# Weights from float64: the sign by a slope of ScalarE, every low part on VectorE

## The chip, the cores and the metric

The kernel runs on one core of a Trainium2 chip. The metric is the device time of one execution, in microseconds. PE is TensorE, DVE is VectorE, ACT is ScalarE, POOL is GpSimd, SP is SyncE, whose queue issues all the transfers here.

## What is computed

A banded attention of 4 batches and 8 heads (576 positions of 64), half of the heads with a dilation of 4, then two feed-forward layers over the 2304 tokens. Cut to what matters:

```
scores = q @ k.T / 8, masked to a band of 32 positions (heads 4 to 7: every 4th of 128)
x = softmax(scores) @ v                        # 2304 tokens x 512
h = x @ w_in;  x = (h * sigmoid(h)) @ w_out    # 512 -> 2048 -> 512
out = (((x @ w1) * (x @ w2)) @ w3) @ w_out2    # 512 -> 1024 -> 1024 -> 512
```

The inputs q, k, v are float32, the weights float64; the result is float32.

## The kernel before

**Products.** A float32 product is made of three faster ones: each operand is split into a high part of fewer bits and a low part (what is missing), and hi*hi, lo*hi and hi*lo are accumulated in PSUM. `split` does it for activations: ACT copies the high part (L452), DVE subtracts (L453).

**Weights.** [...] `Convert` turns a piece of 128 x 512 numbers into float32 by its bits, in a pipeline of stages that are queued as single entries:

- `load`: SP brings the raw piece, 512 KB (L365), into one of four buffers.
- `rebias`: ACT takes the high words (sign, exponent, top of the mantissa) as if they were float32, and multiplies them in place by 2 to the power of -112 (L375), which puts the exponent right.
- `bits`: DVE shifts the high word left by 3 and masks off the sign bit (L383), ORs the sign back in (L387), and ORs in the top three bits of the low word (L391). The float32 number y is done, in one of two buffers.
- `high`: ACT rounds y into the high part, in the weights' place wf (L400).
- `low`: the low part, y minus the high part. For the first layer (`cv`), a piece of odd number goes to POOL (L407), one of even number to DVE (L409). `cv` holds w_in and w_out in turn, so its even pieces are those named i (w_in), its odd ones u (w_out). `cv2`, the second layer's pieces, has them all on DVE.

`fill` queues the entries of the next piece: the low part of an earlier piece, the high part of another, the three bit operations, and the next rescaling, six in all. `micro` takes one entry from the queue, `step` all of them, `need` as many as are wanted for a piece to be complete.

**Order.** The program is emitted in an order that strings of letters set. `START` goes before the first chunk: 12 units of attention (a unit is two blocks of 96 queries for two heads), with conversion entries between. Then come five chunks of tokens through the first layer, with a slot for each of the 16 feature tiles; `SLOT[c]` orders a slot of chunk c. In a slot, h and H are the halves of the next slot's first product (L522, 12 matmuls), t is its nonlinearity (ACT's Tanh, L532, then DVE, L533), g its split, x and X the second product (L550, 12 matmuls); a is a step of the attention, m a conversion entry, c a whole step. Chunk 0 converts two pieces a slot, i and u of a tile; chunks 3 and 4 begin with the second layer's.

A unit of attention runs through these steps, each behind the last: scores on PE (L187), mask and maximum on DVE (L203, 4 instructions with 4 reads of the accumulator), exponentials on ACT (L215, 4), sums and reciprocal on DVE (L223, L225), the normalise on POOL (L227), 4 transposes on PE (L235), their copy on ACT (L241), the product with v on PE (L250, 8 records), and the split into xT (ACT L260, DVE L261).

An engine executes its instructions in the order of the program. `fill` and `low` are where the change lies:

```
if low < high:
    self.queue.append(lambda: self.low(low))
if high < i and high <= self.gate:
    self.queue.append(lambda: self.high(high))
if i < len(self.todo) and i < self.nl + 2:
    self.queue += [lambda x=x: self.bits(i, x) for x in range(3)]
    self.queue.append(lambda: self.rebias(i + 1))
```

Of the kernel before, what the change touches and what calls it, by code (L numbers as in the profile page):

```python
# [17 lines left out]
P = 128  # L18
B, H, S, D = 4, 8, 576, 64
NPAIR = H // 2              # heads go in pairs: 128 partitions of (head, d)  # L20
DM, DFF, DF2 = 512, 2048, 1024
NT = B * S
WIN = 32                    # band width, in (class-ordered) positions
DIL = 4
CL = S // DIL               # positions of a class of a dilated head
QB = 96                     # queries of an attention block
NU = S // (2 * QB)          # units (two blocks) of a pair of heads
PER_B = NPAIR * NU
NUNIT = B * PER_B
KW = 224                    # keys of a unit  # L30
# [3 lines left out]
RING = 1280                 # tokens that xT holds  # L34
CH1 = [(0, 512), (512, 512), (1024, 256), (1280, 512), (1792, 512)]
CH2 = [(0, 512), (512, 512), (1024, 512), (1536, 512), (2048, 256)]
R2 = [0, 512, 0, 512, 1024]  # where a chunk of the second layer lies in xT

# The order of emission. A step of the attention is a group of operations, each with the
# lag (in units) at which it runs behind the first one:  # L40
#   Q split q and k   S scores   M mask and maximum   E exp   N normalise   T transpose
#   W evacuate the transposes   V product with v   O output into xT   K, L load k, v
ATT0 = "S0W2|M0V2|L2T1|K0E0|N0|O2"    # first batch
ATT = "Q0L4K2S1|M1T2|W2E1|V2N1O2"
# Before the first chunk, then in a slot (a feature tile) of each chunk of the first layer:
#   a a step of the attention      m c a part of, a whole step of converting weights
#   h H halves of the next slot's first product     t g its nonlinearity, and its split
#   x X halves of this slot's second product        w W halves of a group of w3 @ wo2
# [10 lines left out]
SPLIT_FROM = 28             # from this unit on the scores are float32r products too  # L59
# [3 lines left out]
# float32 products: each operand is split into hi + lo, two float32r values of  # L63
# 12 significant bits, and hi*hi + lo*hi + hi*lo is accumulated in float32.
# The weights come as float64: their bits are turned into float32 on chip.
# [3 lines left out]
def tile_kernel(  # L69
# [36 lines left out]
    def f32(ap):  # L106
        return ap.bitcast(F32)

    # ---------------------------------------------------------------- masks
    # blocks:  A first block | B inside | C class edge inside | D class edge in front  # L110
    # order of the tile: A B B A C B D
    def build_masks():
# [8 lines left out]
        for i in range(7):  # L121
            lead = 0 if i in (0, 3) else WIN   # 0 <= qi - (kj - lead) < WIN
            keep(mask[:, i, :], lead, 1, -1, P)
            keep(mask[:, i, :], WIN - 1 - lead, -1, 1, P)
        edge = CL - QB                         # class edge inside block 1 (and 4)
# [6 lines left out]
    # ---------------------------------------------------------------- attention  # L132
# [123 lines left out]
    def a_out(n):  # L256
# [6 lines left out]
        def place(a, n_):  # L263
            """cut positions a .. a + n_ of all batches where the ring ends"""
            first = min(n_, RING - a % RING)
            return [(0, first, a % RING)] + ([(first, n_ - first, 0)] if first < n_ else [])

# [31 lines left out]
    def attention_steps():  # L299
        """The steps of the attention, pipelined over units: lists of (operation, unit)."""  # L300
# [12 lines left out]
    class Stream:  # L313
        def __init__(self):
            self.steps, self.at, self.out = attention_steps(), 0, 0
            self.limit = 2 * PER_B          # units whose place in xT is free
# [20 lines left out]
    # ---------------------------------------------------------------- weights  # L337
    # wf[i], first layer: [w_in hi | w_in lo | w_out hi | w_out lo], 512 each
    def quarter(i, k):
        """hi and lo, half k of wf[i]: [P, 2, 512]"""  # L340
# [8 lines left out]
    class Convert:  # L349
        """float64 pieces [P, 512] -> float32 -> hi, lo; a pipeline of four stages."""  # L350

        def __init__(self):
            self.todo = []
            self.nb = self.nh = self.nl = 0     # the next piece of a stage
            self.gate = 1 << 30                 # the last piece whose place is free
# [14 lines left out]
        def rebias(self, i):  # L370
            if i < len(self.todo):
                self.load(i)
                h = self.raw[i][:, :, 1].bitcast(F32)
                # the exponent's offset: 1023 - 127 = 112 * 8, and tiny values go to zero
                nc.scalar.activation(h, h, AF.Copy, scale=2.0 ** -112)  # L375

        def bits(self, i, x):
# [4 lines left out]
            if x == 0:  # L382
                nc.vector.tensor_scalar(  # L383
                    y, hw, 3, 0x7FFFFFF8, op0=ALU.logical_shift_left, op1=ALU.bitwise_and
                )
            elif x == 1:
                nc.vector.scalar_tensor_tensor(  # L387
                    y, hw, -2147483648, y, op0=ALU.bitwise_and, op1=ALU.bitwise_or
                )
# [12 lines left out]
        def low(self, i):  # L402
            if 0 <= i < len(self.todo):
                dst, y = self.parts(i)
                del self.y[i]
                if self is cv and i % 2 == 1:
                    nc.gpsimd.tensor_tensor(dst[:, 1], y, f32(dst[:, 0]), op=ALU.subtract)  # L407
                else:
                    nc.vector.tensor_sub(dst[:, 1], y, f32(dst[:, 0]))  # L409
# [5 lines left out]
        def fill(self):  # L415
# [9 lines left out]
            if i < len(self.todo) and i < self.nl + 2:  # L425
                self.queue += [lambda x=x: self.bits(i, x) for x in range(3)]
# [23 lines left out]
    def split(dst, src):  # L450
        """dst [P, 2, n] <- hi, lo of src [P, n]"""
# [404 lines left out]
```

## Time and profile before

| | |
|---|---|
| median of 3 runs | 866.56 us (866.12 to 867.43) |
| span of the profiled execution, first to last instruction | 864.9 us |
| PE busy | 830.7 us, 96% of the span |
| DVE busy | 454.9 us, 53% |
| ACT busy | 362.0 us, 42% |
| POOL busy | 85.1 us, 10% |
| TensorE's granted clock, mean | 0.999 of full speed (2.4 GHz) |

Of the profiled execution only the span is known; the median of the runs lies 1.7 us above it, which is the time around the instructions. A share of busy time is an average over stages: a stage of its own has to be read in a stretch of the trace.

In the rows below, times count from the span's start. A line of the timeline is: start, duration, engine, line of the kernel, operation, output<-input, shapes, how many instructions are merged, and in brackets how long the engine was idle before and what ended that. A stretch is: length, then for each engine the busy time (instructions), then the granted clock, the share of the transfer engines and GB/s. PEld is PE's loading of weights, which overlaps its matmuls. A group of instructions by form is: line, engine, operation, names, shapes, count, then busy time in us, mean ns of one, and idle time before them. The rows of a tile give the shortest, median and longest duration in ns, and the first and last start.

### The profile page before, as it was taken

The numbers are of one execution on the slowest core, as the hardware profiler recorded it, in microseconds if no ns is written. First come the engines' busy times: TensorE is split into PE (matmuls) and PEld (weight loads), VectorE is DVE, ScalarE is ACT, GpSimd is POOL, SyncE is SP. The second block draws the span as 40 slices with busy tenths as digits, with TensorE's granted clock in tenths as the row PEclk, the third lists the DMA queues.
The fourth block names the chain that finished last, engine by engine and source line by source line (L and its number), as shares of the span: only waits on it lengthen the run. The fifth ranks groups of instructions, "written<-read, shape, count | busy, mean of one in ns | idle before, by whom it ended". The sixth has DMA issues, their size and how long they took to land.

```text
span 864.9 us, 12029 instructions
## 1 busy us (share of the span) xinstructions
PE 830.7 (96%) x4312; PEld 682.5 (79%) x4312; DVE 454.9 (53%) x1141; ACT 362.0 (42%) x962; POOL 85.1 (10%) x86
## 2 busy tenths in 40 slices
PE   5698989899999999999999999999999999999998
PEld 3476666677788999888888888888888888888897
DVE  4789999755552665323267786797123123122121
ACT  5965757465552765222244453454112112121121
POOL 4423232211100121000000000000000000000000
PEclk9999999999999999999999999999999999999999
DMA  6664445131110310300043344351030030020010
GB/s 182 181 196 158 157 159 172 34 118 48 48 43 7 103 42 8 121 1 1 1 170 115 105 147 158 134 184 60 0 98 1 1 97 1 1 74 0 1 49 25
DMA packets 42492, 69.21 MB, mean 80 GB/s; under 512 B 5312, under 2 KB 24768, under 8 KB 42432
## 3 DMA queue, kind: packets, MB, share of 16 engines
q1 hardware_dynamic: 42432, 68.44, 24.8%
q8 instruction: 34, 0.56, 0.2%
q14 instruction: 26, 0.21, 0.1%
HBM read 58.98 MB, written 9.44 MB: 79 GB/s over the span
## 4 chain that ended last, share of the span: by engine, by line
PE 81%; DVE 10%; issue 3%; DMA 2%; ACT 2%; SPq 1%; POOL 0%; ACTq 0%; DVEq 0%; POOLq 0%
PE ab L598 23%; PE x L550 19%; PE h L522 18%; PE o L628 11%; PE wp L501 5%; PE s L182 2%; DVE y_i L391 2%; ACT sm L215 2%; PE o L250 1%; DMA v<-in_v_dram 1%; DVE sm L203 1%; DVE t L533 1%; PE t L235 1%; DVE y_i L387 1%; DVE y_u L387 1%
## 5 line engine op out<-in xcount | busy, mean ns | idle before, releaser
L522 PE MATMUL h<-xT,wf 128*128 128x512 f32 (+1 forms) x960 | 221.3, 375 | 1.4 <-DVE wf L409 1.4
L550 PE MATMUL x<-g,wf 128*128 128x512 f32 (+1 forms) x960 | 214.1, 370 | 0.0
L598 PE MATMUL ab<-xT,wf 128*128 128x512 f32 (+1 forms) x960 | 203.7, 368 | 0.0
L598 PEld LDWEIGHTS ab<-xT,wf 128*128 128x128 f32 x960 | 168.2, 188 | 30.6
L522 PEld LDWEIGHTS h<-xT,wf 128*128 128x128 f32 x960 | 166.2, 189 | 31.6 <-DVE wf L409 2.2
L550 PEld LDWEIGHTS x<-g,wf 128*128 128x128 f32 x960 | 167.2, 188 | 30.2
L609 DVE TENSOR_TENSOR pa<-pa,ab 128x512 f32<-128x512 f32 (+1 forms) x40 | 25.4, 635 | 183.5 <-PE ab L598 183.5
L533 DVE SCALAR_TENSOR_TENSOR t<-t,h 128x512 f32<-128x512 f32 (+1 forms) x80 | 50.6, 632 | 114.6 <-ACT t L532 114.4
L628 PE MATMUL o<-wf,pg 128*128 128x512 f32 x432 | 104.4, 390 | 0.0
L628 PEld LDWEIGHTS o<-wf,pg 128*128 128x128 f32 x432 | 80.6, 188 | 16.4
L532 ACT ACTIVATE t<-h 128x512 f32<-128x512 f32 (+1 forms) x80 | 43.8, 548 | 96.0 <-PE h L522 93.9
L227 POOL TENSOR_TENSOR sm<-sm,rs 96x512 f32<-96x512 f32 x48 | 60.3, 1256 | 239.4 <-DVE rs L225 162.3
L215 ACT ACTIVATE sm<-sm,nm 96x128 f32<-96x128 f32 x192 | 74.4, 390 | 5.7 <-DVE nm L203 5.6
L608 ACT ACTIVATE pa<-ab 128x512 f32<-128x512 f32 (+1 forms) x40 | 22.2, 554 | 117.2 <-PE ab L598 117.2
L453 DVE TENSOR_TENSOR g<-t,g 128x512 fp32r<-128x512 f32 (+1 forms) x80 | 54.3, 679 | 30.9 <-ACT g L452 29.8
L452 ACT ACTIVATE pg<-pa 128x512 fp32r<-128x512 f32 (+1 forms) x40 | 23.6, 589 | 103.1 <-DVE pa L609 103.1
L452 ACT ACTIVATE g<-t 128x512 fp32r<-128x512 f32 (+1 forms) x80 | 46.8, 585 | 31.9 <-DVE t L533 31.9
L203 DVE CUSTOM_DVE_ANT_0 sm<-s,mask 96x128 f32<-96x128 f32 x192 | 43.8, 280 | 5.9 <-PE s L187 5.8
L235 PE MATMUL t<-ident,sm 96*128 96x96 f32 x192 | 25.7, 257 | 19.5 <-POOL sm L227 19.5
L501 PE MATMUL wp<-wf,xT 128*128 128x512 f32 x192 | 43.9, 389 | 0.0
L235 PEld LDWEIGHTS t<-ident,sm 96*128 96x128 f32 x192 | 19.7, 143 | 29.2 <-POOL sm L227 27.1
L501 PEld LDWEIGHTS wp<-wf,xT 128*128 128x128 f32 x192 | 36.0, 188 | 7.5
(66 smaller groups left out, 690.5 us busy)
## 6 DMA issues: line engine op xcount, KB each, us to landing
raw_i<-in_w_in_dram SPq DMA_DIRECT2D x16, 512.0 KB, 3.4
raw_u<-in_w_out_dram SPq DMA_DIRECT2D x16, 512.0 KB, 3.4
raw<-in_w_dram SPq DMA_DIRECT2D x16, 512.0 KB, 3.2
raw_w<-in_w_dram SPq DMA_DIRECT2D x16, 512.0 KB, 3.3
v<-in_v_dram SPq DMA_DIRECT2D x96, 64.0 KB, 2.4
kz<-in_kT_dram SPq DMA_DIRECT2D x96, 56.0 KB, 2.3
q<-in_qT_dram SPq DMA_DIRECT2D x16, 288.0 KB, 2.8
x2d<-x2s SPq DMA_DIRECT2D x8, 512.0 KB, 3.2
```

What stands on the lines that cost most here:

```text
L203: nc.vector.tensor_tensor_reduce(sm[:, c, h], s_ps[:QB, c, h], mask[:, mo + c], -SCALE, 3.0e38, ALU.add, ALU.min, nm[:, 2 * c + h:2 * c + ...
L215: nc.scalar.activation(sm[:, c, h], sm[:, c, h], AF.Exp, bias=nm[:, j:j + 1], scale=-1.0, accum_out=su[:, j:j + 1],)
L227: nc.gpsimd.tensor_tensor(f, f, rs.to_broadcast([QB, 4, P]), op=ALU.mult)
L235: nc.tensor.transpose(t_v[:, j], sm[:, j // 2, j % 2], ident[:QB, :QB])
L452: nc.scalar.activation(dst[:, 0], src, AF.Copy)
L453: nc.vector.tensor_sub(dst[:, 1], src, f32(dst[:, 0]))
L501: nc.tensor.matmul(wp_ps[i], a[:, i // 2, sa, i % 2 * P:(i % 2 + 1) * P], o[:, sb], start=(jt == 0 and x == 0), stop=(jt == NG - 1 and x = ...
L522: nc.tensor.matmul(ps, win(f, sa, kt), xT[:, kt, sb, r0:r0 + n], start=(kt == 0 and x == 0), stop=(kt == KT - 1 and x == 2),)
L533: nc.vector.scalar_tensor_tensor(t, t, 1.0, ps, op0=ALU.add, op1=ALU.mult)
L550: nc.tensor.matmul(xps[c][m][:, :n], wout(f, sa, m), g[:, sb], start=(f == 0 and sa == 0 and sb == 0), stop=(f == NF - 1 and sb == 1),)
L598: nc.tensor.matmul(ps[:, :n], w12(j, x, sa, kt), xT[:, kt, sb, r:r + n], start=(kt == 0 and y == 0), stop=(kt == KT - 1 and y == 2),)
L628: nc.tensor.matmul(ops[c][m], g[:, sa, m * P:(m + 1) * P], wp_v(j, sb), start=(j == 0 and sa == 0 and sb == 0), stop=(j == NG - 1 and sa = ...
```

## The change

The sign goes another way. ACT's rescaling is a Prelu: a value of at least zero gets the slope 1, a negative one the slope 2 to the power of 32. So the rescaled high word of a negative weight has an exponent larger by 32, and that bit is the one which the shift by 3 brings to the place of the sign. The mask and the OR with the sign are gone; `bits` has two entries a piece in place of three, and `fill` queues five in place of six. And `low` of the first layer's odd pieces goes from POOL to DVE.

```diff
         def rebias(self, i):
-                nc.scalar.activation(h, h, AF.Copy, scale=2.0 ** -112)
+                nc.scalar.activation(h, h, AF.Prelu, scale=2.0 ** -112, alpha=2.0 ** 32)
         def bits(self, i, x):
             if x == 0:
-                nc.vector.tensor_scalar(
-                    y, hw, 3, 0x7FFFFFF8, op0=ALU.logical_shift_left, op1=ALU.bitwise_and
-                )
-            elif x == 1:
-                nc.vector.scalar_tensor_tensor(
-                    y, hw, -2147483648, y, op0=ALU.bitwise_and, op1=ALU.bitwise_or
-                )
+                nc.vector.tensor_single_scalar(y, hw, 3, op=ALU.logical_shift_left)
             else:
         def low(self, i):
-                if self is cv and i % 2 == 1:
-                    nc.gpsimd.tensor_tensor(dst[:, 1], y, f32(dst[:, 0]), op=ALU.subtract)
-                else:
-                    nc.vector.tensor_sub(dst[:, 1], y, f32(dst[:, 0]))
+                nc.vector.tensor_sub(dst[:, 1], y, f32(dst[:, 0]))
         def fill(self):
-                self.queue += [lambda x=x: self.bits(i, x) for x in range(3)]
+                self.queue += [lambda x=x: self.bits(i, x) for x in range(2)]
```

Comments are gone too, so lines have other numbers after it: the rescaling is L376 (was L375), the shift L384 (L383), the OR with the low word L386 (L391), the high part L395 (L400), the low part L401 (L409), the split L444 and L445 (L452, L453), Tanh and what follows L524 and L525 (L532, L533).

**DVE, a steady slot of chunk 0.** The numbers behind a name count the feature tile and the buffer: y_i7 is the converted piece i of tile 7, raw its raw data, t and g the nonlinearity and its split, sm a unit's masked scores. Before:

```order
L533 SCALAR_TENSOR_TENSOR t_0_5_1136<-t_0_5_1136,h_0_5_1083 128x512 [waits Activation_49]
L383 TENSOR_SCALAR y_i7_1140<-raw_i7_1067 128x512 [waits DMAHW5_49,DVE_49]
...
L225 RECIPROCAL rs_17_1148<-su_17_1124 96x4 [waits DVE_49]
L261 TENSOR_TENSOR xT_109<-o_16_1142,xT_109 128x4x48 [waits Activation_49]
L387 SCALAR_TENSOR_TENSOR y_i7_1140<-raw_i7_1067,y_i7_1140 128x512
L391 SCALAR_TENSOR_TENSOR y_i7_1140<-raw_i7_1067,y_i7_1140 128x512 [waits DVE_49]
L453 TENSOR_TENSOR g_0_5_1158<-t_0_5_1136,g_0_5_1158 128x512 [waits Activation_49]
L203 ISA sm_18_1177,nm_18_1178<-s_18_1166,mask_111 96x128 [waits PE_49]
...
L383 TENSOR_SCALAR y_u7_1195<-raw_u7_1113 128x512 [waits DMAHW3_49,Pool_49]
L387 SCALAR_TENSOR_TENSOR y_u7_1195<-raw_u7_1113,y_u7_1195 128x512 [waits DVE_49]
L391 SCALAR_TENSOR_TENSOR y_u7_1195<-raw_u7_1113,y_u7_1195 128x512 [waits DVE_49]
L409 TENSOR_TENSOR wf7_100<-y_i7_1140,wf7_100 128x512 [waits Activation_49]
```

The same slot with the change:

```order
L525 SCALAR_TENSOR_TENSOR t_0_5_1130<-t_0_5_1130,h_0_5_1078 128x512 [waits Activation_49]
L384 TENSOR_SCALAR y_u7_1134<-raw_u7_1062 128x512 [waits DMAHW6_49,DVE_49]
...
L225 RECIPROCAL rs_17_1142<-su_17_1118 96x4 [waits DVE_49]
L261 TENSOR_TENSOR xT_109<-o_16_1136,xT_109 128x4x48 [waits Activation_49]
L386 SCALAR_TENSOR_TENSOR y_u7_1134<-raw_u7_1062,y_u7_1134 128x512
L445 TENSOR_TENSOR g_0_5_1151<-t_0_5_1130,g_0_5_1151 128x512 [waits Activation_49]
L401 TENSOR_TENSOR wf7_100<-y_i7_1104,wf7_100 128x512
L203 ISA sm_18_1170,nm_18_1171<-s_18_1159,mask_111 96x128 [waits PE_49,Pool_49]
...
L384 TENSOR_SCALAR y_i8_1188<-raw_i8_1107 128x512 [waits DMAHW4_49,DVE_49]
L386 SCALAR_TENSOR_TENSOR y_i8_1188<-raw_i8_1107,y_i8_1188 128x512 [waits DVE_49]
L401 TENSOR_TENSOR wf7_100<-y_u7_1134,wf7_100 128x512 [waits Activation_49]
```

The u piece has moved to the place around xT, the i piece of the next tile to the place behind the maxima; g stands directly behind the one OR that is left, and both low parts are in the slot.

**ACT, just ahead of chunk 0 and into it.** h_0_0 is the first product of chunk 0, raw_u2 the raw data of piece u of tile 2; at and xT belong to the attention. Before:

```order
L400 ACTIVATE wf1_94<-y_u1_595 128x512 [waits DVE_49]
L260 ACTIVATE xT_109<-o_10_660 128x192 [waits PE_49]
L241 ACTIVATE at_11_681<-t_11_676 128x384 [waits PE_49,Activation_49]
L215 ACTIVATE sm_12_670,su_12_683<-sm_12_670,nm_12_671 96x128 [waits DVE_49] x4
L260 ACTIVATE xT_109<-o_11_688 128x192 [waits PE_49]
L375 ACTIVATE raw_u2_630<-raw_u2_630 128x512 [waits DMAHW7_49]
L532 ACTIVATE t_0_0_717<-h_0_0_704 128x512 [waits PE_49]
```

With the change:

```order
L395 ACTIVATE wf2_95<-y_i2_631 128x512 [waits DVE_49]
L260 ACTIVATE xT_109<-o_10_662 128x192 [waits PE_49]
L241 ACTIVATE at_11_683<-t_11_678 128x384 [waits PE_49,Activation_49]
L215 ACTIVATE sm_12_672,su_12_685<-sm_12_672,nm_12_673 96x128 [waits DVE_49] x4
L260 ACTIVATE xT_109<-o_11_690 128x192 [waits PE_49]
L376 ACTIVATE raw_i3_634<-raw_i3_634 128x512 [waits DMAHW0_49]
L524 ACTIVATE t_0_0_720<-h_0_0_707 128x512 [waits PE_49]
```

By the first Tanh the conversion is one piece further: the high part of i2 in place of u1, the rescaling of i3 in place of u2. In all, ACT has 5 high parts and 7 rescalings ahead of that Tanh, where it had 4 and 6. Of ACT's table there is one load in the order, ahead of the first rescaling, before and with the change.

## Rows read from the trace of the kernel before

**Rows 1.** Busy time of the engines in three stretches, from chunk 0 on

```profile
100.00:125.00 25.00, 22.00 (x119) 16.37 (x118) 24.62 (x58) 15.43 (x48) 8.44 (x6) 1.00 0.49 163
...
175.00:200.00 25.00, 25.00 (x146) 19.64 (x145) 13.80 (x55) 15.53 (x54) 3.12 (x3) 1.00 0.31 95
...
550.00:600.00 50.00, 50.00 (x222) 41.38 (x221) 41.98 (x70) 23.45 (x40) 0.00 (x0) 1.00 0.38 126
```

**Rows 2.** Timeline of PE, chunk 0 and the first slots behind it

```profile
52.68 2.88 PE L550 MATMUL x<-g,wf 128*128 128x512 f32 x12
...
110.56 0.37 PEld L235 LDWEIGHTS t<-ident,sm 96*128 96x128 f32 x4 [1.42 <-POOL sm L227]
...
155.31 2.90 PE L550 MATMUL x<-g,wf 128*128 128x512 f32 x12
...
159.13 2.79 PE L522 MATMUL h<-xT,wf 128*128 128x512 f32 x11 [0.70 <-DVE wf L409]
...
165.55 2.83 PE L522 MATMUL h<-xT,wf 128*128 128x512 f32 x11 [0.68 <-DVE wf L409]
168.22 1.52 PE L550 MATMUL x<-g,wf 128*128 128x512 f32 x6
...
175.64 1.52 PE L550 MATMUL x<-g,wf 128*128 128x512 f32 x6
```

**Rows 3.** Timeline of DVE, a steady slot of chunk 0

```profile
108.93 0.68 DVE L387 SCALAR_TENSOR_TENSOR y_i<-raw_i,y_i 128x512 int32<-128x512 int32 x1
109.64 2.65 DVE L391 SCALAR_TENSOR_TENSOR y_i<-raw_i,y_i 128x512 int32<-128x512 int32 x1
112.22 0.68 DVE L453 TENSOR_TENSOR g<-t,g 128x512 fp32r<-128x512 f32 x1
...
113.66 0.41 DVE L383 TENSOR_SCALAR y_u<-raw_u 128x512 int32<-128x512 int32 x1
114.11 0.69 DVE L387 SCALAR_TENSOR_TENSOR y_u<-raw_u,y_u 128x512 int32<-128x512 int32 x1
114.84 0.69 DVE L391 SCALAR_TENSOR_TENSOR y_u<-raw_u,y_u 128x512 int32<-128x512 int32 x1
115.45 0.69 DVE L409 TENSOR_TENSOR wf<-y_i,wf 128x512 fp32r<-128x512 f32 x1
116.05 0.68 DVE L533 SCALAR_TENSOR_TENSOR t<-t,h 128x512 f32<-128x512 f32 x1
...
117.52 0.68 DVE L387 SCALAR_TENSOR_TENSOR y_i<-raw_i,y_i 128x512 int32<-128x512 int32 x1
```

**Rows 4.** Timeline of POOL, the same slot

```profile
108.93 1.57 POOL L227 TENSOR_TENSOR sm<-sm,rs 96x512 f32<-96x512 f32 x1 [5.78 <-DVE rs L225]
110.47 1.27 POOL L407 TENSOR_TENSOR wf<-y_u,wf 128x512 fp32r<-128x512 f32 x1
```

**Rows 5.** Instructions on the tile y_i, whole span

```profile
L383 DVE TENSOR_SCALAR y_i<-raw_i x16: 394/420/1451, 10.4 to 159.6; 128x512 int32<-128x512 int32 x16
...
L391 DVE SCALAR_TENSOR_TENSOR y_i<-raw_i,y_i x16: 657/2656/2664, 16.7 to 161.8; 128x512 int32<-128x512 int32 x16
```

**Rows 6.** Groups of ACT's instructions by form, whole span

```profile
L532 ACT ACTIVATE t<-h 128x512 f32<-128x512 f32 x64 | 37.8, 590 | 84.2 <-PE h L522 84.2
...
L608 ACT ACTIVATE pa<-ab 128x512 f32<-128x512 f32 x32 | 19.1, 597 | 101.7 <-PE ab L598 101.7
...
L375 ACT ACTIVATE raw_i<-raw_i 128x512 f32<-128x512 f32 x16 | 10.5, 658 | 5.9 <-DMA raw_i<-in_w_in_dram 5.9
...
L375 ACT ACT_TABLE_LOAD x1 | 1.3, 1283 | 0.7 <-PEq L844 0.7
```

**Rows 7.** Timeline of ACT, first exponentials of three units before chunk 0

```profile
29.14 0.40 ACT L215 ACTIVATE sm<-sm,nm 96x128 f32<-96x128 f32 x1 [0.36 <-DVE nm L203]
...
31.75 0.40 ACT L215 ACTIVATE sm<-sm,nm 96x128 f32<-96x128 f32 x1 [0.37 <-DVE nm L203]
...
34.96 0.39 ACT L215 ACTIVATE sm<-sm,nm 96x128 f32<-96x128 f32 x1
```

## The prediction

> **What bounds the kernel now.** I read the table by stretch first [rows 1]: engine busy time, stretch by stretch. From 175 us on PE is busy in every microsecond, and around 550 to 600 us it stays so although VectorE (DVE) works 42 of 50 us there. What VectorE saves after 175 us therefore hides behind PE and is worth nothing. Between 100 and 125 us it is the other way round: DVE is busy 24.62 of 25 us, PE 22.00, ScalarE (ACT) 15.43. That is chunk 0 of the first layer, where the weights are converted just ahead of their use, two pieces a slot.
>
> Then PE's instructions in order of time [rows 2]. The first slot of chunk 0 starts its second product (x) at 52.68 us, the thirteenth at 155.31, the fifteenth at 168.22. In the steady slots the weight loads of the transposes wait 1.42 us for POOL; in two late slots, without attention, PE waits 0.70 and 0.68 us for DVE's L409. The slot from 168.22 to 175.64 has the same matrix work as a steady one (12 h, 12 x, the 4 transposes, 8 o and 4 s records of a unit) and no such wait: 7.42 us. That is PE's own pace, and what a slot falls to if nothing else binds.
>
> Then DVE's instructions of one slot [rows 3], which run without a gap: from L387 at 108.93 to the same place a slot later, 117.52, is 8.59 us. One row is out of scale: L391 of an i piece takes 2.65 us, L391 of the u piece 0.69. POOL's rows show why [rows 4]. The normalise (L227) becomes ready beside L387, and takes 1.57 us; at its end POOL goes on with L407, the low part of a u piece, 1.27 us, until 111.74. L391 ends 0.55 us after that, as if it ran only then. It is not one slot: L391 has a median of 2656 ns over the 16 i pieces, and L383, which reads only one tensor, once reached 1451 against a median of 420 [rows 5]. I read it so that a running POOL operation holds back the DVE operation on SBUF behind it.
>
> **The change part by part.** All terms for a steady slot, as distances from start to start in [rows 3], since DVE's instructions overlap a little.
>
> Removed on DVE: L387 of both pieces, 108.93 to 109.64 and 114.11 to 114.84. Removed on POOL: L407. Added on DVE: one low part for the u piece, as L409: 115.45 to 116.05, 0.60. Moved, since a piece now has one entry less in the queue of conversion steps: the place behind xT (L261), where POOL's normalise starts, now belongs to the u piece, and the next two-tensor operation behind it is g (old L453), followed by the low part of i.
>
> The new DVE slot: t to the place behind xT, 116.05 to 117.52, 1.47. The OR with the low word takes the place of L387 beside the start of the normalise: 0.71. Then g meets the normalise, without L407 behind it: POOL ends 1.57 after its start, g ends 0.55 later, and its successor starts where its own row would let it, so g costs 1.33 instead of 0.60. Low part of i 0.60; the four maxima 0.84 (112.22 to 113.66 less g's 0.60); shift 0.45; OR 0.61; low part of u 0.60. Sum 6.61 us instead of 8.59. If xT comes late, the normalise is over before g, and it is 5.88.
>
> So DVE falls below PE's 7.42, and the slot becomes PE's: the saving is 1.17, not 1.98. From 52.68 to 155.31 are 12 slots, 102.63 us; 12 x 7.42 is 89.0: **13.6 us** gained. In the two late slots the waits of 0.70 and 0.68 end with L387: **1.4 us**.
>
> ACT: Copy becomes Prelu in the rescaling, two a slot. ACT has 15.43 of 25 us, 5.30 a slot; 2.1 us are free at PE's pace. No row has a Prelu. As bounds: Tanh against Copy at 128x512 out of PSUM, 590 and 597 [rows 6], so nothing; at most another 0.66, the whole rescaling twice. Even that gives 6.6 a slot, under 7.42. I take nothing, as Tanh is the nearest row of a function that is not Copy.
>
> The Trainium skill ("ScalarE: Activation LUTs", What ACT_TABLE_LOAD costs) charges about 93 ns for each per-partition pointer operand; if Prelu's bias and slope came so, two in a slot would add 0.37 us to ACT, and the sum would stay but for about 1.3 us over 7 rescalings before chunk 0. No run here shows it.
>
> The shift with one operation in place of two: 0.42 as L383, at worst the 0.69 of a two-tensor OR; twice 0.27 makes DVE 7.15, still under PE. Nothing.
>
> The start, before chunk 0. Here ACT paces the attention units: 2.61 us from one unit's first exponential to the next without conversions, 3.21 with two [rows 7], so 0.30 for one. The shorter queue brings conversions forward: the order of ACT has 12 of them ahead of the first Tanh, against 10. Between 0.30 and their whole length of 0.66 each, 0.6 to 1.3: I take **0.9 us** lost. One more load of 512 KB is issued in this time, which could delay a load of keys: from nothing to 3.2 us (512 KB at the 163 GB/s of the stretch from 100 us) [rows 1]; I take **0.3**, since ACT, not a load, paces the units that I read.
>
> The second layer's 40 pieces lose an operation each on DVE beside a PE that is busy throughout: nothing. If that cover were gone, they would be 40 x 0.69, 28 us.
>
> Sum: 13.6 + 1.4 - 0.9 - 0.3 = 13.8. The profiled execution has a span of 864.9 us, so 851.1; the median of the runs, 866.56, lies 1.7 above the span, hence **852.8 us**.
>
> **The rivals.**
>
> A: the transposes' wait for POOL stays in part. The normalise waits for a sum, that for ACT's exponentials, those for DVE's maxima, and all three engines work in order; xT, which now stands between two steps of the same piece, waits for PE. For it: the transposes are what PE waits for now. Against it: DVE has 0.8 us to spare, ACT 2.1. If half of the 1.17 us that a slot should lose stays, 12 x 0.585 is 7.0: 859.8; if all, 866.4.
>
> B: PE runs closer than in the slot I took it from. Without the wait of the weight loads, a steady slot is 8.59 - 1.42 = 7.17, and x takes its 12 products in one run in chunk 0, in two runs of 6 later. And the two conversions at the start could vanish in gaps. 12 x 0.25 + 1.2 gives 848.6. I count it as the forecast's lower side.
>
> C: the change is slower, through ACT's tables. ACT now alternates Exp, Tanh, Copy and Prelu. If Prelu is not among the functions loaded with the others, each rescaling brings two loads of the table at 1.28 us [rows 6]: four a slot, 5.13, so ACT takes 10.43 and becomes the bound; it decides from 8.59 on, which is 0.82 a load. Then 12 x 1.84 us are lost in chunk 0 instead of 13.6 gained, and some 18 us (7 x 2 x 1.28) at the start: about 906 us, or more if chunks 3 and 4 also feel it. Against it: ACT's compiled order has one table load, at its head, and loads are instructions of their own in the trace.
>
> The Trainium skill (the same page, Table sets) has one load for every switch to a function of another set, and does not name Prelu among those it lists with Exp; by it the compiled order would show the loads, so this stays unlikely.
>
> D: no change, since something else holds a slot at about 8.5, such as the loads: chunk 0 then saves nothing, and the start's 1.2 us are lost: 867.8. Against it: PE's waits in chunk 0 name POOL and DVE, no load [rows 2], and DVE works without a gap [rows 3].
>
> **How the numbers follow.** The forecast with its lower side 0.68, A 0.24, C 0.03, D 0.03, the rest 0.02. The range goes from 848.5, which is B, to 860, which takes in A up to its half; above it lie A in full, C and D. Some 0.2% of this time, 1.7 us, is what a measurement can tell from no change; A in full and D lie within it, and only C and D's worse cases above. So faster 0.94, same 0.03, slower 0.03.
>
> **What would show it.** Right: between 60 and 150 us DVE is no longer busy throughout but 79 to 90%, PE without the wait for POOL; x starts come every 7.4 us; no L391-like row of 2.6 us in steady slots, but a g of about 1.4 at most; the first x starts 1 us later. Wrong: a slot near 8 with a wait of PE for POOL or ACT (A); table loads in ACT's rows (C); a slot near 8.5 and an engine that waits for a load (D). A Prelu row much above 0.66 us would make the ACT term wrong, and a shift of 0.69 the DVE sum, without moving the time.

## The result, and the profile after

The changed kernel takes 853.66 us in the median of four runs (852.29 to 855.22), the kernel before 866.99 in the same session (866.12 to 867.94): a ratio of 0.9841, 95% interval 0.9825 to 0.9858. The forecast was 852.8, its range 848.5 to 860.0. The execution whose profile is shown has 855.22 us and a span of 853.2, so it is 11.7 us shorter than the profiled one of before.

Of the page, the busy time of the engines over the whole span, and the shares of the chain that ended last:

```profile
PE 830.0 (97%) x4312; PEld 685.8 (80%) x4312; DVE 395.6 (46%) x1085; ACT 363.8 (43%) x962; POOL 58.6 (7%) x70
...
PE 95%; ACT 3%; DVE 1%; issue 0%; DMA 0%; POOL 0%; SPq 0%; POOLq 0%; ACTq 0%
```

VectorE lost 59.3 us of work, POOL 26.5, and the kernel only 11.7. PE has as much to do as before; what went is PE's waiting, and PE's own work is now nearly the whole chain (95%, before 81%).

PE in order of time, chunk 0 and the two late slots behind it (to compare with [rows 2]):

```profile
49.04 4.25 PE L514 MATMUL h<-xT,wf 128*128 128x512 f32 x12
...
57.12 2.88 PE L542 MATMUL x<-g,wf 128*128 128x512 f32 x12
...
99.68 0.49 PE L235 MATMUL t<-ident,sm 96*128 96x96 f32 x4
...
145.74 2.90 PE L542 MATMUL x<-g,wf 128*128 128x512 f32 x12
...
151.21 2.88 PE L542 MATMUL x<-g,wf 128*128 128x512 f32 x12
...
156.65 1.52 PE L542 MATMUL x<-g,wf 128*128 128x512 f32 x6
```

The x of the first slot starts at 57.12 us, that of the thirteenth at 145.74: 88.62 us for 12 slots, 7.39 each, against 102.63 and 8.55. The transposes wait for nobody. The two late slots take 10.91 us together (145.74 to 156.65) in place of 12.91. So 14.0 and 2.0 us were gained. But the first x stood at 52.68 before: 4.4 us were lost ahead of it. 14.0 + 2.0 - 4.4 = 11.6, which is the difference of the spans, 11.7, but for 0.1.

VectorE and POOL in a steady slot (to compare with [rows 3, 4]):

```profile
105.22 0.36 DVE L261 TENSOR_TENSOR xT<-o,xT 128x192 fp32r<-128x192 f32 x1 [1.15 <-ACT xT L260]
105.49 0.68 DVE L386 SCALAR_TENSOR_TENSOR y_u<-raw_u,y_u 128x512 int32<-128x512 int32 x1
106.30 0.69 DVE L445 TENSOR_TENSOR g<-t,g 128x512 fp32r<-128x512 f32 x1
```

```profile
104.23 1.04 POOL L227 TENSOR_TENSOR sm<-sm,rs 96x512 f32<-96x512 f32 x1 [6.35 <-DVE rs L225]
```

VectorE now waits 1.15 us for xT, and in that time POOL's normalise runs alone: 1.04 us, where beside VectorE it took 1.57. It ends at 105.27, ahead of the OR and of g, which take their plain 0.68 and 0.69.

Four stretches of the changed kernel (columns as in [rows 1]):

```profile
40.00:45.00 5.00, 3.10 (x29) 2.07 (x29) 4.28 (x18) 4.89 (x20) 1.73 (x3) 0.99 0.51 144
45.00:50.00 5.00, 4.36 (x18) 3.09 (x19) 1.57 (x12) 2.67 (x12) 0.93 (x1) 0.50 0.95 290
50.00:55.00 5.00, 5.00 (x20) 3.94 (x19) 2.77 (x5) 1.39 (x3) 1.30 (x1) 0.83 0.61 205
...
100.00:125.00 25.00, 25.00 (x136) 19.62 (x134) 20.75 (x70) 19.45 (x60) 3.11 (x3) 1.00 0.61 198
```

And of the kernel before, one of these stretches and its first 12 h:

```profile
45.00:50.00 5.00, 4.65 (x26) 3.75 (x27) 3.52 (x11) 3.19 (x12) 2.60 (x2) 1.00 0.86 244
```

```profile
45.83 3.02 PE L522 MATMUL h<-xT,wf 128*128 128x512 f32 x12
```

From 100 to 125 us PE is full and DVE busy 83%. At 45 to 50 us the granted clock is 0.50, which is 1.2 GHz: the 12 h that start at 49.04 take 4.25 us, before 3.02. Before, the clock was 1.00 in all four stretches.

And the place in the start that lost most among the units, the tenth: VectorE, POOL, and the first exponential behind them.

```profile
35.08 1.48 DVE L386 SCALAR_TENSOR_TENSOR y_u<-raw_u,y_u 128x512 int32<-128x512 int32 x1
36.48 0.28 DVE L203 CUSTOM_DVE_ANT_0 sm<-s,mask 96x128 f32<-96x128 f32 x1
```

```profile
34.97 1.04 POOL L227 TENSOR_TENSOR sm<-sm,rs 96x512 f32<-96x512 f32 x1 [1.94 <-DVE xT L261]
```

```profile
36.79 0.40 ACT L215 ACTIVATE sm<-sm,nm 96x128 f32<-96x128 f32 x1 [1.57 <-DVE nm L203]
```

An OR starts 0.11 us behind the normalise, takes 1.48 in place of 0.69, and the maxima stand behind it. ScalarE, which paces this part, is idle for 1.57 us. The exponentials of this unit start 4.37 us after those of the unit before (32.42), where before it was 3.21 [rows 7].

### The profile page after: what moved, and what is told of

Its sections match the earlier page's. It is cut to its first block, busy times and chain, and to the rows that moved or that the text cites. A ratio compares the mean times of both kernels' runs of the same rounds, so it can differ in the third digit from the quotient of the medians.

```text
span 853.2 us, 11956 instructions
## 1 busy us (share of the span) xinstructions
PE 830.0 (97%) x4312; PEld 685.8 (80%) x4312; DVE 395.6 (46%) x1085; ACT 363.8 (43%) x962; POOL 58.6 (7%) x70
## 4 chain that ended last, share of the span: by engine, by line
PE 95%; ACT 3%; DVE 1%; issue 0%; DMA 0%; POOL 0%; SPq 0%; POOLq 0%; ACTq 0%
PE h L514 24%; PE x L542 23%; PE ab L590 23%; PE o L620 12%; PE wp L493 5%; PE s L187 2%; PE o L250 2%; PE s L182 2%; ACT sm L215 2%; PE t L235 2%; DMA raw_i<-in_w_in_dram 0%; ACT at L241 0%; POOL sm L227 0%; DVE sm L203 0%; DVE kz L648 0%
## 5 line engine op out<-in xcount | busy, mean ns | idle before, releaser
L525 DVE SCALAR_TENSOR_TENSOR t<-t,h 128x512 f32<-128x512 f32 (+1 forms) x80 | 50.7, 634 | 128.0 <-ACT t L524 127.4
L524 ACT ACTIVATE t<-h 128x512 f32<-128x512 f32 (+1 forms) x80 | 43.9, 548 | 104.9 <-PE h L514 102.7
L227 POOL TENSOR_TENSOR sm<-sm,rs 96x512 f32<-96x512 f32 x48 | 53.8, 1120 | 264.0 <-DVE rs L225 171.4
L445 DVE TENSOR_TENSOR g<-t,g 128x512 fp32r<-128x512 f32 (+1 forms) x80 | 54.4, 680 | 33.6 <-ACT g L444 31.3
L444 ACT ACTIVATE pg<-pa 128x512 fp32r<-128x512 f32 (+1 forms) x40 | 23.6, 589 | 103.4 <-DVE pa L601 103.4
L444 ACT ACTIVATE g<-t 128x512 fp32r<-128x512 f32 (+1 forms) x80 | 46.8, 585 | 29.7 <-DVE t L525 29.6
L203 DVE CUSTOM_DVE_ANT_0 sm<-s,mask 96x128 f32<-96x128 f32 x192 | 43.8, 280 | 6.6 <-PE s L187 6.6
L187 PE MATMUL s<-kz,q 128*96 128x256 f32 x112 | 33.7, 431 | 4.6 <-DMA kz<-in_kT_dram 4.6
L445 DVE TENSOR_TENSOR pg<-pa,pg 128x512 fp32r<-128x512 f32 (+1 forms) x40 | 25.6, 640 | 26.3 <-ACT pg L444 26.3
```

The source lines that it names most:

```text
L187: nc.tensor.matmul(s_ps[:QB, c], t[:, QB * i:QB * i + QB], kz[n % 3][:, :, k0:k0 + P], start=True, stop=True,)
L227: nc.gpsimd.tensor_tensor(f, f, rs.to_broadcast([QB, 4, P]), op=ALU.mult)
L444: nc.scalar.activation(dst[:, 0], src, AF.Copy)
L445: nc.vector.tensor_sub(dst[:, 1], src, f32(dst[:, 0]))
L524: nc.scalar.activation(t, ps, AF.Tanh, scale=0.5)
L525: nc.vector.scalar_tensor_tensor(t, t, 1.0, ps, op0=ALU.add, op1=ALU.mult)
```

## The experiments

The theory: chunk 0 gained because VectorE's sum fell below PE's 7.39 us a slot; the start lost because conversion work met POOL's normalise ahead of the maxima, and because the clock fell. Each kernel that follows is the whole change but for its edit, unless another base is named. x1 stands for the start of the first x. Medians of before were 867.71, 866.83 and 867.44 in the three sessions.

**The sign by the slope alone.**

```diff
-                nc.vector.tensor_sub(dst[:, 1], y, f32(dst[:, 0]))
+                if self is cv and i % 2 == 1:
+                    nc.gpsimd.tensor_tensor(dst[:, 1], y, f32(dst[:, 0]), op=ALU.subtract)
+                else:
+                    nc.vector.tensor_sub(dst[:, 1], y, f32(dst[:, 0]))
```

> The change with the odd low parts back on GpSimd: the sign by the slope alone. Theory (a slot of the first chunk was held by VectorE's sum, in which the sign's OR was 0.69 and the overlap with GpSimd's half only stretched single operations): VectorE's sum of a slot is about 0.6 us below that of the kernel with all low parts on VectorE, so TensorE keeps its own pace of 7.4 us a slot, and the time is that of the whole change, 852 to 856 us. Rival (what held the slot was the chain through GpSimd: with the half low part there TensorE waits for GpSimd again): most of the stall of about 1.1 us a slot stays, the slot is 8.0 us or more, and the time 860 to 866 us.

Measured: 855.92 us, ratio 0.9869 (0.9851 to 0.9888). The slots are 7.39 us but for the first, 9.20. Timeline of PE, and of POOL in the first two slots:

```profile
57.08 2.90 PE L545 MATMUL x<-g,wf 128*128 128x512 f32 x12
...
64.48 0.55 PE L235 MATMUL t<-ident,sm 96*128 96x96 f32 x4 [1.60 <-POOL sm L227]
...
66.28 2.89 PE L545 MATMUL x<-g,wf 128*128 128x512 f32 x12
...
73.66 2.90 PE L545 MATMUL x<-g,wf 128*128 128x512 f32 x12
```

```profile
61.66 2.77 POOL L227 TENSOR_TENSOR sm<-sm,rs 96x512 f32<-96x512 f32 x1 [4.50 <-DVE rs L225]
...
69.10 1.04 POOL L227 TENSOR_TENSOR sm<-sm,rs 96x512 f32<-96x512 f32 x1 [3.43 <-DVE rs L225]
```

And VectorE in the second slot:

```profile
70.06 0.36 DVE L261 TENSOR_TENSOR xT<-o,xT 128x192 fp32r<-128x192 f32 x1 [1.14 <-ACT xT L260]
```

The theory holds in 11 slots of 12, the rival in one: there the normalise met the OR, g and a low part, took 2.77 us, and the transposes waited 1.60. In the second slot VectorE is early, waits 1.14 us for xT, and the normalise runs alone meanwhile, so that the meeting is over. In the kernel before, VectorE had no such gap, and PE waited for POOL in every slot [rows 2].

**All low parts on VectorE alone** (on the kernel before):

```diff
-                if self is cv and i % 2 == 1:
-                    nc.gpsimd.tensor_tensor(dst[:, 1], y, f32(dst[:, 0]), op=ALU.subtract)
-                else:
-                    nc.vector.tensor_sub(dst[:, 1], y, f32(dst[:, 0]))
+                nc.vector.tensor_sub(dst[:, 1], y, f32(dst[:, 0]))
```

> The kernel before with all low parts on VectorE and the sign still placed by an OR there. Theory (VectorE's time in a slot ended it, and most of GpSimd's half low part costs VectorE as much or more through the stretched operations beside it): a slot of 8.59 us loses 1.27 us of stretched work and gains 0.60 us, 7.9 us, still set by VectorE; about 8 us less over twelve slots, 857 to 860 us. Rival 1 (only VectorE's own operations count, and GpSimd's half cost it nothing): 0.6 us a slot more, about 874 us. Rival 2 (the wait for GpSimd was all): the slot falls to TensorE's pace, 7.4 us, and the time is that of the whole change or below, 850 to 855 us.

Measured: 859.04 us, ratio 0.9909 (0.9891 to 0.9927); x at 60.78 and every 7.95 us behind it, x1 at 53.21. The OR with the low word of the i pieces (to compare with [rows 5]):

```profile
L391 DVE SCALAR_TENSOR_TENSOR y_i<-raw_i,y_i x16: 657/1412/1415, 15.4 to 153.0; 128x512 int32<-128x512 int32 x16
```

So taking work off POOL and giving it to VectorE, which was the bound, gains by itself: without POOL's L407 behind the normalise this OR loses 1.24 us (a median of 1412 ns in place of 2656), and the low part costs 0.60, which leaves the 0.64 by which a slot got shorter. The two halves alone gain 11.8 and 8.7 us, the whole change 13.3: not the sum, since what the second can add ends at PE's 7.39.

**Copy in place of Prelu.**

```diff
-                nc.scalar.activation(h, h, AF.Prelu, scale=2.0 ** -112, alpha=2.0 ** 32)
+                nc.scalar.activation(h, h, AF.Copy, scale=2.0 ** -112)
```

> The whole change, with Copy in place of Prelu in the rescaling of the first operand's high words (this leaves out the sign of negative weights). Theory (Prelu costs ScalarE what Copy does): the time is that of the change within 1 us, and one table load stands in the trace in both. Rival (Prelu's slope has a price that lies on the chain of the start): 1 to 4 us below the change, with the first product of the second matmul of a tile earlier by as much.

Measured: 852.92 us (852.21 to 855.55), against 853.66 for the change: the same. ScalarE's groups by form, the change first, then this kernel:

```profile
L376 ACT ACTIVATE raw_i<-raw_i 128x512 f32<-128x512 f32 x16 | 10.7, 672 | 5.6 <-DMA raw_i<-in_w_in_dram 5.6
...
L376 ACT ACT_TABLE_LOAD x1 | 1.3, 1283 | 0.7 <-PEq L836 0.7
```

```profile
L376 ACT ACTIVATE raw_i<-raw_i 128x512 f32<-128x512 f32 x16 | 10.7, 669 | 5.8 <-DMA raw_i<-in_w_in_dram 5.8
```

Prelu costs 3 ns more than Copy on the i pieces (on the u pieces both take 676), and the one table load stands in both. This profile tells something else: the order of instructions is that of the change, yet x1 is at 54.77, not 57.12, and the clock is 1.00 in every stretch of the start. A unit's product with v that PE starts at 42.00 us here starts at 41.73 in the change; from there to x1 are 12.77 us here and 15.39 there. So the fall of the clock cost 2.6 us in the profiled execution of the change, 2.35 of the start's 4.4 once its earlier beginning is taken off, and the order cost 2.1.

**Another order of the start.** The string `START` is written anew, and nothing else: conversion entries come evenly, so that VectorE's stand between a unit's maxima and the next sums, and none between xT and the maxima.

```diff
-START = "aaaaamaaaaaamaaamamamaaaaaaammaaaaammamaaaaammaaa"
+START = "aaammaaaaaaammaaammaaamaaamaaamaaammaaamaaamaaamaaammaaamaaamaaamaaammaaamaaamaaamaaammaaamaaamaaaaaaaaaaaaaa"
```

> The whole change with another order of the steps ahead of the first chunk: the conversion's steps are spread evenly over the units, so that no OR on VectorE stands right behind the output's low part, where it met GpSimd's normalise, and none ahead of a maximum. Theory (the start's 4.4 us come from such a meeting, which delays the maxima by 0.8 to 1.5 us, empties TensorE and lets its granted clock fall to 0.5 at 45 to 50 us): no exp of a unit is more than 3.4 us behind the one before, the clock of 45 to 50 us is above 0.8, the first product of the second matmul starts 2 to 4 us earlier than the 57.1 us of the change, and the time is 850 to 852 us. Rival (the start loses by the number of conversions and loads, not by their places): the first one still starts at 56 to 58 us, and the time is 853 to 855 us.

Measured: 849.70 us (849.47 to 850.50), ratio 0.9798 (0.9781 to 0.9815). x1 is at 52.36. ACT's timeline, the first exponentials of the ninth to eleventh unit, and two stretches:

```profile
31.27 0.40 ACT L215 ACTIVATE sm<-sm,nm 96x128 f32<-96x128 f32 x1
...
34.33 0.39 ACT L215 ACTIVATE sm<-sm,nm 96x128 f32<-96x128 f32 x1
...
37.12 0.40 ACT L215 ACTIVATE sm<-sm,nm 96x128 f32<-96x128 f32 x1
```

```profile
40.00:45.00 5.00, 2.47 (x21) 1.76 (x22) 2.85 (x18) 3.26 (x14) 1.43 (x2) 1.00 0.70 220
45.00:50.00 5.00, 5.00 (x28) 4.00 (x29) 3.12 (x8) 3.46 (x13) 1.30 (x1) 1.00 0.94 271
```

From 31.27 to 34.33 are 3.06 us, the longest step from the fourth unit to the twelfth (only the one to the third unit, 4.00, is over the theory's 3.4). The rival falls: ScalarE has 14 conversions ahead of the first Tanh here, 12 in the order of the change, and is still earlier. x1 is 4.8 us earlier than in the profile of the change, 2.4 earlier than in the profile of Copy, which has the order of the change without the fall. It is the fastest of all, and its interval lies wholly below that of the change.

**The change once more**, unedited.

> The whole change itself once more, in the same session as the three that follow. Theory (of the 4.4 us that the start lost in the profiled execution, some 2.3 are a fall of TensorE's granted clock to 0.5 within 45 to 55 us that comes in some executions and not in others; the other 2.1 are the order's): where the profile of this execution shows a clock of 1.00 in 45 to 55 us the first product of the second matmul starts at 54.5 to 55.0 us and the span is 850 to 851.5 us; where it shows the fall, 56.5 to 57.5 us and 852.5 to 853.5. Rival (the fall belongs to this order and comes each time): 57 us again.

Measured: 853.84 us (853.61 to 854.88). x1 is at 55.47, which neither side had: with a clock of 1.00 in 45 to 55 us, as here, the theory asked for 54.5 to 55.0. The clock fell again, elsewhere:

```profile
40.00:45.00 5.00, 3.93 (x20) 2.54 (x20) 3.23 (x16) 4.03 (x19) 1.03 (x1) 0.67 0.47 119
45.00:50.00 5.00, 3.98 (x30) 2.82 (x31) 2.60 (x15) 3.58 (x14) 1.57 (x1) 1.00 0.96 281
```

There PE has less to do than in the stretch behind, and x1 is 0.7 us later than with Copy. So the fall is not tied to one place, and with this order and ScalarE's Prelu or Copy it came in two profiles of three.

**The spread order with fewer conversions.** The same string without the later entries of the conversion.

> The evenly spread order, with the conversions stopped after the ninth unit of the start: 11 of ScalarE's conversions stand ahead of the first Tanh in place of 15. Theory (what costs in the start is where a conversion meets the attention's chain; four conversions fewer free about 2.4 us of ScalarE, whose idle time there is already over 1 us a unit): the first product of the second matmul starts 0 to 1 us earlier than in the evenly spread order, and the time is 848.5 to 850.5 us. Rival (the number decides): 2 us or more earlier, 846 to 848 us. Second rival (the pieces are then short in the first chunk, whose slots convert only two each): some slots of the first chunk stretch and the time is 851 us or more.

Measured: 850.73 us (849.85 to 852.73); x1 at 52.30, the slots 7.39. The first theory, 0.2 us above its upper bound: four conversions fewer (10 in place of 14; the counts in the expectation take in the table load's row) make x1 0.06 us earlier. In this order, then, the number does not matter. Two of its five executions took 852.6 and 852.7 us at a mean clock of 0.991 and 0.993, the other three 849.9 to 850.7 at 0.999: this order does not keep the clock up in every execution.

**One more operation a slot.** The OR with the low word is done twice, for the odd pieces (first) or for all (second):

```diff
+                for _ in range(1 + (self is cv and i % 2)):
...
+                for _ in range(1 + (self is cv)):
```

> The whole change, with the low word's OR done twice for each odd piece: one more operation of 0.60 us on VectorE in each slot of the first chunk. Theory (a slot is the larger of TensorE's own 7.39 us and VectorE's sum, 5.88 us with the normalise over ahead of the second split's subtraction, 6.61 us with the two beside each other; 6.5 to 7.2 us with this operation): the slots stay at 7.39 us, and the time at 852 to 856 us. Rival (any operation more on VectorE brings the meeting with the normalise back and, with it, the slot of the kernel before): slots of 7.9 us or more, 859 us or more.

> The whole change, with the low word's OR done twice for every piece: two more operations of 0.60 us on VectorE in each slot of the first chunk, so that VectorE has as much to do as where the sign keeps its own OR. Theory (VectorE's sum is then 6.61 and 1.20, 7.8 us, over TensorE's 7.39): a slot of 7.8 to 8.0 us, set by VectorE, and 857 to 861 us. Rival (VectorE's sum is 5.88 and 1.20, 7.1 us, since the normalise can keep out of the way): slots of 7.39 us, and 852 to 856 us.

Measured: 856.91 us (ratio 0.9883, 0.9867 to 0.9898) and 865.42 (0.9982, 0.9970 to 0.9994). PE's x, twice in the first and twice in the second kernel, with the transposes of the second:

```profile
103.11 2.90 PE L543 MATMUL x<-g,wf 128*128 128x512 f32 x12
...
110.50 2.90 PE L543 MATMUL x<-g,wf 128*128 128x512 f32 x12
```

```profile
102.61 2.88 PE L543 MATMUL x<-g,wf 128*128 128x512 f32 x12
...
108.75 0.55 PE L235 MATMUL t<-ident,sm 96*128 96x96 f32 x4 [0.36 <-POOL sm L227]
...
110.56 2.89 PE L543 MATMUL x<-g,wf 128*128 128x512 f32 x12
```

The slots are as the theory has them: 7.39 us with one operation more (the last 7.52), 7.95 with two (the first 7.57), where VectorE's sum binds again and PE waits for POOL. The times are above what it gave, and in the profiles the excess lies in the start: x1 at 58.81 and at 63.24. There the doubled OR stands just behind xT and meets the normalise; in the second kernel

```profile
38.76 2.21 DVE L387 SCALAR_TENSOR_TENSOR y_u<-raw_u,y_u 128x512 int32<-128x512 int32 x2
```

with the maxima behind it, and a clock of 0.66 from 30 to 40 us and 0.50 from 50 to 55. This execution is the slowest of its ten (868.09 us, the median 865.42), so what it shows of the start may be up to 2.7 us worse than usual.

**Two more operations, in the spread order.**

> Both the low word's OR done twice for every piece and the evenly spread order of the start. Theory (the doubled OR cost the start 8 us only because it stood between the output's low part and the maxima; in the spread order it stands behind the maxima, where VectorE waits for the sums): the first product of the second matmul starts at 52 to 53.5 us in place of 63.2, the slots of the first chunk stay at 7.95 us, and the time is 849.7 + 12 x 0.56 = 856.4, between 855.5 and 858.5 us. Rival (the start pays for VectorE's operations wherever they stand): the first one starts at 57 us or later, and the time is 860 us or more.

Measured: 861.21 us (861.12 to 862.58). The slots are 7.95 us; x1 is at 56.60, between the two: 6.6 us earlier than in the order of the change, 4.2 later than in the spread order without the doubled OR. Of these 4.2, 1.5 are longer units (the twelfth unit's exponentials at 41.63 in place of 40.17); the rest comes with a clock of 0.51 at 45 to 50 us. These profiles seem to say that the place is most of it. The medians do not: the doubled OR adds 11.5 us in this order (849.70 to 861.21) and 11.8 in that of the change (853.66 to 865.42), in both 6.7 for the slots (12 x 0.56) and some 5 for the start. So the time goes with the rival: the start paid about as much in either order, here mostly through the clock. The theory's time was 5 us too low. What the spread order gains over that of the change, 4.0 us, it keeps with the doubled OR (4.2).

**The slope alone, in the spread order.**

> The sign by the slope, the odd low parts on GpSimd, and the evenly spread order of the start: what the low parts' place is worth when the start no longer meets it. Theory (with the sign's OR gone a slot of the first chunk keeps TensorE's pace wherever the odd low part is made): slots of 7.39 us, and 849.5 to 851.5 us, as with all of them on VectorE. Rival (the first slots fall into the meeting again, with the transposes waiting for GpSimd as at 64.5 us of the slope alone): one slot or more of 8 us or above, 851.5 to 855 us.

Measured: 855.52 us (852.72 to 855.98). The rival: three slots of twelve take 8.40, 8.57 and 8.58 us, the others 7.39. One of the three, PE, then POOL, then VectorE:

```profile
99.85 2.90 PE L545 MATMUL x<-g,wf 128*128 128x512 f32 x12
...
106.62 0.55 PE L235 MATMUL t<-ident,sm 96*128 96x96 f32 x4 [0.97 <-POOL sm L227]
...
108.42 2.90 PE L545 MATMUL x<-g,wf 128*128 128x512 f32 x12
```

```profile
96.43 1.04 POOL L227 TENSOR_TENSOR sm<-sm,rs 96x512 f32<-96x512 f32 x1 [5.68 <-DVE rs L225]
97.43 1.28 POOL L402 TENSOR_TENSOR wf<-y_u,wf 128x512 fp32r<-128x512 f32 x1
104.39 2.17 POOL L227 TENSOR_TENSOR sm<-sm,rs 96x512 f32<-96x512 f32 x1 [5.68 <-DVE rs L225]
```

```profile
96.53 2.73 DVE L386 SCALAR_TENSOR_TENSOR y_i<-raw_i,y_i 128x512 int32<-128x512 int32 x1
...
104.39 0.68 DVE L386 SCALAR_TENSOR_TENSOR y_i<-raw_i,y_i 128x512 int32<-128x512 int32 x1
104.99 0.68 DVE L448 TENSOR_TENSOR g<-t,g 128x512 fp32r<-128x512 f32 x1
105.59 0.28 DVE L203 CUSTOM_DVE_ANT_0 sm<-s,mask 96x128 f32<-96x128 f32 x1
```

At 96.43 POOL was first by 0.10 us, and VectorE's OR took 2.73, through both of POOL's operations; VectorE has room for that, and the slot stays at PE's pace. At 104.39 both started together, VectorE went first, the normalise waited through the OR and g, and PE's transposes for the normalise. What hurts a slot here, where VectorE has room, is not VectorE held by POOL but POOL held by VectorE. With the low parts all on VectorE, no slot of chunk 0 had this in the change, in its repetition or in the two spread orders, where every normalise of these slots takes 1.03 or 1.04 us; where VectorE had no room (the low parts alone, the OR done twice for all pieces) each took 1.57 or 1.58 again. So that half of the change is worth some 3.4 us in this profile (3 x 1.1), 1.8 in the first experiment; the remaining 2.2 us against the spread order are an x1 at 54.53, with a clock of 0.71 and 0.60 from 40 to 50 us. The one execution at a mean clock of 0.999 took 852.72, which is 3.0 above the spread order.

## Why the prediction was right, point by point

- **The slot of chunk 0.** Right. PE's own pace was taken from a slot behind chunk 0, 7.42 us; it is 7.39, and the 12 slots gave 14.0 us where 13.6 were forecast. The 7.17 of rival B and another bound, as in D, did not come.
- **VectorE's sum.** Right in what it decides. Of its two cases, 6.61 and 5.88, the second came: xT waits for PE's products with v, the normalise is over, and g takes 0.69, not 1.33. Two operations more make a slot of 7.95, with the normalise at 1.57 again: 7.95 - 1.20 is 6.75, nearer to 6.61. So, by an estimate from these, VectorE has about 0.6 us of room a slot: one operation, not two.
- **The reading of L391's 2.65 us.** Right, and shown by taking L407 away: 1.41 in place of 2.65 in the second experiment. The Trainium skill (SBUF — State Buffer, Who interferes with whom) says that a VectorE instruction with two SBUF inputs and a GpSimd instruction that reads SBUF hold a shared port for their whole length, and that the order of issue decides which one waits. The traces agree: 2.73 us of VectorE where POOL was first by 0.10 us, 2.17 us of POOL where it was not, while L203 ran its 0.28 beside it. The prediction used only the half in which VectorE waits.
- **The late slots.** 2.0 us in place of 1.4: the waits of 0.70 and 0.68 ended, and the slots, 5.47 and 5.44 us, are 0.6 shorter than before beyond that.
- **Prelu.** Its term of nothing was right: 672 ns against 669 for Copy in the same order. The charge for pointer operands that the prediction cited, two of about 93 ns, does not show. Rival C's table loads are not there.
- **The start.** Here a term was mis-sized: 1.2 us forecast, 4.4 in the profiled execution. The step that failed counted ScalarE's conversions ahead of the first Tanh and priced each at 0.30 to 0.66. The spread order has two more of them and loses nothing. What was lost went by place: the shorter queue moved an OR behind xT and in front of the maxima (1.2 us at the tenth unit, 4.37 against 3.21); 1.0 went over the units before it, which was not traced to single places but came back with the spread order; and 2.35 went by the clock, on which the prediction has nothing (the units behind the tenth won 0.2 back). The meeting had been read in chunk 0 and was looked for there alone. The 0.3 us for a late load of keys shows in no row: between 8 and 50 us PE waits for no load.
- **The sum.** Of the profiled execution the span was forecast at 851.1 and is 853.2: the gains were put 1.0 us too low, the loss 3.2. The median, 853.66, is only 0.9 from the forecast, and that is partly luck: without the fall the loss is 2.1, 0.9 more than forecast, which the gains just cancel (the profile of Copy has a span of 850.9). The other three executions of the change had a mean clock of 0.997 in place of 0.992; where it fell in them is not recorded.

What decides whether the clock falls in the start stays open. It is at 0.71 or below in some stretch of 40 to 55 us in the profiles of the change, of its repetition and of five of the nine other kernels, and at 1.00 in those of Copy, of the low parts alone, and of both spread orders without a further edit. What PE did just before does not decide it alone: from 28 to 45 us PE's waits are the same within 0.02 us in the profiles of the change and of Copy (the longest 1.61 us, for ScalarE), and the clock fell in the first only. The Trainium skill (TensorE: Matmul & The Clock Gate, HAM oscillation) has a TensorE that idles between groups of matmuls fall to the lower clock; the traces agree only in part, as with equal waits of 1.61 us and less it fell in one and not in the other. It was not tried apart.

## What to carry to other kernels

Moving work off a co-processor onto the engine that is the bound can pay, where the two hold each other up: count what an operation costs beside its neighbour, not alone. Once the bound has moved to another engine, look where the other operations land when a queue gets shorter: here one slid in front of a chain without slack, and 2 to 4 of 16 us were lost until the start's order was written anew (849.70 us). And price a removed operation by the room that it leaves, for the second of two halves adds little once the floor is reached.

## What the runs showed of the hardware

- The same instructions of VectorE and POOL ran a slot in two ways. In the slope alone the first slot had a normalise of 2.77 us, the eleven behind it 1.04; in the spread order of the same kernel, where the i piece stands beside xT, three slots of twelve went wrong, each four behind the last. Who starts first goes with it: in the four slots that went wrong VectorE's OR begins with the normalise or 0.01 us ahead of it (61.65 and 61.66, 73.65 and 73.66, 104.39 twice, 135.13 and 135.14); at 96.43 POOL was 0.10 ahead, and the slot kept its pace.
- An operation of 0.6 us, done once more at each of six places in the start of the change, cost the start some 5 us by the medians, more than the 3.6 of the operations themselves: the meetings lengthened the units, and then the clock at 1.2 GHz PE's work.
- A fall of the clock costs by where it lies. In the profile of the change it was at 0.58 and 0.74 from 10 to 20 us too, and from the first unit's exponentials to the twelfth's are 34.02 us, as in Copy's, where it was 1.00 (34.01); the fall at 45 to 50 us, where PE has its first h, cost 2.6.
